# A fused attention and feed-forward kernel: output tiles of the last block brought forward, evictions shared, eight transposing loads

## Chip, cores, metric

One NeuronCore of a Trainium2 chip. The metric is the device time of the core in microseconds (us), lower is better. A "tail" below is the time from the end of the last exponential on ScalarE to some later event.

## What is computed

x is 2048 x 512 in bf16. There are 32 heads of size 16, and a feed-forward width of 1792.

```python
g = sigmoid((x * gate_w).sum(-1, keepdims=True))
a = attention(x, wqkv) @ wo                      # softmax(q k^T / 4) v, 32 heads
b = (silu(x @ w_gate) * (x @ w_up)) @ w_down
out = g * a + (1 - g) * b
```

## The kernel before: the parts concerned

The kernel orders the instructions of TensorE (PE), VectorE (DVE) and ScalarE (ACT) at build time, by planned costs. Of every 16 key tiles in a "unit" (four heads, 512 queries) most go to ScalarE as exponentials, and some to VectorE, which computes exp with arithmetic on bit patterns (y_t). The kernel uses eight banks of PSUM: two pairs for scores, one for o_ps (the product with v), three for everything else.

```python
# loads: nine transposing DMAs
parts = [(0, 2 * QBW, dc) for dc in range(DC)] + [(2 * QBW, S, dc) for dc in range(DC - 1)]
parts += [(2 * QBW, 3 * QBW, DC - 1), (3 * QBW, S, DC - 1)]
for t0, t1, dc in parts:
    nc.sync.dma_start_transpose(out=xT[:, dc, t0:t1], in_=x[t0:t1, dc * P:(dc + 1) * P])
# ...
def gate_end():
    act(out=ge[:, :], in_=ge[:, :], func=ACT.Tanh, scale=0.5)
    def end():                                   # gval = g, omg = 1 - g
        vec.tensor_scalar(out=gval[:, :], in0=ge[:, :], scalar1=1.0, scalar2=0.5, op0=ALU.add, op1=ALU.mult)
        vec.tensor_scalar(out=omg[:, :], in0=ge[:, :], scalar1=-0.5, scalar2=0.5, op0=ALU.mult, op1=ALU.add)
    later(0.4, end, plan.act + 0.2)              # 0.4: the planned cost
# ... in down_pieces: bblk = omg * (feed-forward product)
# ... in next_pv: emit_pv(pv_list(None)[0])      # ScalarE blocks first, then y_t blocks

def tail(k):       # k = 0: just ahead of the last product with v; k = 1: behind it
    if k == 0:
        a_ps.extend(m_tile("a_l")[:, :] for _ in range(2))
        al = ps_s.tile([P, 2 * QBW], F32, tag="s", name="al")
        a_ps.extend([al[:, 0:QBW], al[:, QBW:2 * QBW]])
    todo = [(tq, b) for tq in range(TQ) for b in range(NB - 1)]        # 12 products
    for tq, b in todo[:11] if k == 0 else todo[11:]:
        mm(a_ps[tq][:, 0:D], lhsT=onc[QB - 1][:, b, tq * P:(tq + 1) * P], rhs=wo_t[:, b, :], ...)
# ... the end of the program
tail(1)
last_mm(0, osbs[un - 1])        # four products
# dt: sums of the last unit's heads; reciprocal; rps: broadcast; on_l = osb * rps
last_mm(1, on_l)                # four products
for tq in range(TQ):            # mt = a_ps * gval + bblk on VectorE, then a store on SP
    store((QB - 1) * TQ + tq, a_ps[tq], bblk[:, tq, :], mt[:, tq, :])
```

## Time and profile before

| | before |
|---|---|
| median of the first three runs | 847.9 us (847.81 to 848.98) |
| span of the profiled execution | 846.8 us |
| first exponential starts / last one ends | 18.66 / 834.92 us |
| tail, last exponential's end to the end | 11.9 us |

The end of the last exponential is the start and duration of the last `e_t` line of the timeline.

```profile
833.69 1.23 ACT L160 ACTIVATE e_t<-s_t 128x1024 bf16<-128x1024 f32 x1
...
833.64 1.17 ACT L160 ACTIVATE e_t<-s_t 128x1024 bf16<-128x1024 f32 x1
```

The profile is to be read with this in mind: between 18.66 and 834.92 ScalarE is busy nearly throughout (800.48 of the 808.40 us from 18.60 to 827.00), so only the head, the tail and the small idle times of ScalarE can give anything.

### The profile page before, as it was taken

The numbers are of one execution on the slowest core, as the hardware profiler recorded it, in microseconds if no ns is written. First come the engines' busy times: TensorE is split into PE (matmuls) and PEld (weight loads), VectorE is DVE, ScalarE is ACT, GpSimd is POOL, SyncE is SP. The second block draws the span as 40 slices with busy tenths as digits, with TensorE's granted clock in tenths as the row PEclk, the third lists the DMA queues.
The fourth block names the chain that finished last, engine by engine and source line by source line (L and its number), as shares of the span: only waits on it lengthen the run. The fifth ranks groups of instructions, "written<-read, shape, count | busy, mean of one in ns | idle before, by whom it ended". The sixth has DMA issues, their size and how long they took to land. (4 is left out here: it accounts for less than half of the span.)

```text
span 846.8 us, 16228 instructions
## 1 busy us (share of the span) xinstructions
PE 764.1 (90%) x6049; PEld 262.5 (31%) x6078; DVE 797.4 (94%) x1160; ACT 813.9 (96%) x910; POOL 93.2 (11%) x122
## 2 busy tenths in 40 slices
PE   7999998999889998889899988898999899989995
PEld 3222233332223333232223322223333223233332
DVE  6999998999999999999999898999998999999995
ACT  3999999999999999999999999999999999999994
POOL 5010100010011011011101000100100110110100
PEclk9999999999999999999999999999999999999999
DMA  9432445345454334454443354444532554553331
GB/s 202 128 66 47 88 77 113 69 93 104 94 112 99 66 80 100 102 113 92 100 99 72 77 115 86 100 102 84 112 73 55 106 110 92 108 105 76 75 66 36
DMA packets 101447, 78.23 MB, mean 92 GB/s; under 512 B 77792, under 2 KB 89656, under 8 KB 101368
## 3 DMA queue, kind: packets, MB, share of 16 engines
q0 software_dynamic: 12672, 46.14, 28.6%
q1 hardware_dynamic: 87112, 30.86, 15.4%
q8 instruction: 47, 0.77, 0.4%
q10 hardware_dynamic: 1584, 0.20, 0.2%
q14 instruction: 32, 0.26, 0.1%
HBM read 20.83 MB, written 2.34 MB: 27 GB/s over the span
## 5 line engine op out<-in xcount | busy, mean ns | idle before, releaser
L160 ACT ACTIVATE e_t<-s_t 128x1024 bf16<-128x1024 f32 x846 | 791.9, 1106 | 8.3 <-PE s_t L157 6.6
L157 PE MATMUL s_t<-qx,kaug 64*128 64x512 bf16 x1376 | 293.9, 381 | 37.7 <-ACT e_t L160 32.5
L166 DVE TENSOR_SCALAR y_t<-d_t 128x512 uint16<-128x512 f32 x356 | 234.6, 682 | 15.8 <-PE d_t L157 13.2
L157 PEld LDWEIGHTS <-kaug 64*128 64x128 bf16 x2048 | 137.0, 93 | 323.8 <-issue 287.9
L157 PE MATMUL o_ps<-e_t,vaug 128*32 128x512 bf16 x1692 | 160.0, 389 | 2.3 <-DVE osb L166 1.0
L157 PE MATMUL gu_a<-xT,wg 64*128 64x512 bf16 x448 | 136.5, 377 | 0.0
L157 PE MATMUL gu_b<-xT,wu 64*128 64x512 bf16 x448 | 134.7, 377 | 1.3 <-DVE y_t L166 0.9
L157 PE MATMUL d_t<-qx,kaug 64*128 64x512 bf16 x288 | 107.6, 378 | 16.3 <-DVE y_t L166 9.2
L157 PEld LDWEIGHTS <-vaug 128*32 128x32 bf16 (+1 forms) x2148 | 46.0, 93 | 148.0 <-issue 146.6
L772 POOL DMA_DIRECT2D y_t<-u_t x44 | 40.1, 912 | 351.7 <-PE s_t L157 211.3
L772 POOL DMA_DIRECT2D y_t<-kaug x38 | 35.9, 946 | 310.3 <-PE s_t L157 191.4
L157 PE MATMUL dps_a<-wd_t,mt 64*128 64x512 bf16 x224 | 65.3, 376 | 0.0
L157 PE MATMUL dps_b<-wd_t,mt 64*128 64x512 bf16 x224 | 64.9, 375 | 0.3 <-DVE y_t L166 0.2
L166 DVE TENSOR_SCALAR z_t<-y_t 128x2048 uint16<-128x2048 uint16 x89 | 61.5, 691 | 2.1
L166 DVE TENSOR_SCALAR y_t<-y_t 128x2048 uint16<-128x2048 uint16 x89 | 60.9, 684 | 2.4 <-DMA y_t<-kaug 1.4
L166 DVE TENSOR_TENSOR u_t<-u_t 128x2048 f16<-128x2048 f16 x44 | 53.8, 1223 | 1.1
L166 DVE TENSOR_TENSOR u_t<-u_t,z_t 128x2048 f16<-128x2048 f16 x44 | 53.5, 1217 | 0.1
L157 PE MATMUL s_t<-q,kaug 64*128 64x512 bf16 x212 | 43.0, 381 | 7.6 <-ACT e_t L160 7.0
L166 DVE TENSOR_TENSOR kaug<-kaug 128x2048 f16<-128x2048 f16 x39 | 47.7, 1223 | 0.9
L166 DVE TENSOR_TENSOR kaug<-kaug,z_t 128x2048 f16<-128x2048 f16 x39 | 47.5, 1218 | 0.1
L157 PEld LDWEIGHTS <-wg 64*128 64x128 bf16 x448 | 40.8, 94 | 20.9 <-issue 9.0
L157 PEld LDWEIGHTS <-wu 64*128 64x128 bf16 x448 | 41.7, 94 | 16.1 <-issue 0.7
(119 smaller groups left out, 626.6 us busy)
## 6 DMA issues: line engine op xcount, KB each, us to landing
y_t<-u_t POOLq DMA_DIRECT2D x44, 512.0 KB, 4.8
y_t<-kaug POOLq DMA_DIRECT2D x38, 512.0 KB, 5.0
wg<-in_B_w_gate_dram SPq DMA_DIRECT2D x56, 128.0 KB
wu<-in_B_w_up_dram SPq DMA_DIRECT2D x56, 128.0 KB
y_t<-wd_t POOLq DMA_DIRECT2D x6, 512.0 KB, 4.6
on<-osb SPq DMA_DIRECT2D x120, 16.0 KB
rb<-rr SPq DMA_DIRECT2D x15, 128.0 KB
wd_t<-in_B_w_down_dram SPq DMA_DIRECT2D x7, 256.0 KB
```

Source lines behind the costliest of these rows:

```text
L157: return ordered(nc.tensor.matmul(*args, **kw))
L160: ordered(nc.scalar.activation(*args, **kw))
L166: return lambda *a, **kw: ordered(f(*a, **kw))
L772: nc.gpsimd.dma_start(out=ya, in_=ua, accum_op=ALU.add)
```

## The change

The intent is to shorten the serial tail. Output tiles 0 and 1 of the last block, with the feed-forward part added by a product with the identity matrix, go out while the last exponentials run. The last product with v is that of the last exponential and no longer a y_t product. Tiles 2 and 3 are split five and five around it. The gate is kept in another form, so that out = g * (a + ((1-g)/g) * b): now the eviction needs one PSUM operand and a scale only, which ScalarE can do too. The loads become eight of one size.

```diff
-    parts = [(0, 2 * QBW, dc) for dc in range(DC)] + [(2 * QBW, S, dc) for dc in range(DC - 1)]
-    parts += [(2 * QBW, 3 * QBW, DC - 1), (3 * QBW, S, DC - 1)]
+    for t0 in (0, 2 * QBW):
+        for dc in range(DC): ...                       # eight loads of 1024 rows
@@ gate_end
-        act(out=ge, in_=ge, func=ACT.Tanh, scale=0.5)
+        act(out=ge, in_=ge, func=ACT.Exp, scale=-1.0)  # ge = exp(-l), gval = 1 / (1 + ge), omg = ge * gval
-        later(0.4, end, plan.act + 0.2)
+        later(0.5, end, plan.act + 0.2)
@@ down_pieces: end
+            share = omg if qb < QB - 1 else ge
@@
+    def last_rows(t):
+        cs = slice(t * P, (t + 1) * P)
+        return lambda i: ((onc[QB - 1][:, i, cs], wo_t[:, i, :]) if i < NB - 1 else
+                          (osbs[UNITS - 2][:, cs], wo_l[:, 0, :]) if i == NB - 1 else (ident[:, :], bblk[:, t, :]))
+    def last_pieces():                                 # tiles 0 and 1: ten pieces of two half-row products
+        return two_banks(NB + 1, "a_l", last_rows(0), last_rows(1), keep, stop=False)
+    def tail(k):
+        todo = [(tq, i) for tq in (2, 3) for i in range(NB + 1)]
+        for tq, i in todo[:5] if k == 0 else todo[5:]: ...
@@ the chain is paced once all its inputs are there
+            pace.add(last_pieces(), SLOTS - KT // 2, SLOTS, prev, cond=ripe)
@@ next_pv
+        ns = pv_list(None)
+        if closed == UNITS - 1 and done_a[closed] == hi[closed] - 1 and vready:
+            ns.reverse()
+        emit_pv(ns[0])
@@ the end
-    for tq in range(TQ):
-        store((QB - 1) * TQ + tq, a_ps[tq], bblk[:, tq, :], mt[:, tq, :])
+        if tq % 2 == 0:
+            vec.tensor_scalar(out=mt[:, tq, :], in0=a_ps[tq][:, 0:D], scalar1=gval[:, t:t + 1], ...)
+        else:
+            act(out=mt[:, tq, :], in_=a_ps[tq][:, 0:D], func=ACT.Identity, scale=gval[:, t:t + 1])
+        (nc.sync if tq % 2 == 0 else nc.scalar).dma_start(out=out_f[...], in_=mt[:, tq, :])
```

More of the change, by code (lines that the diff above doesn't have):

```diff
@@ L171 @@
     xT = big.tile([P, DC, S], BF16, name="xT")
-    parts = [(0, 2 * QBW, dc) for dc in range(DC)] + [(2 * QBW, S, dc) for dc in range(DC - 1)]
-    parts += [(2 * QBW, 3 * QBW, DC - 1), (3 * QBW, S, DC - 1)]
-    for t0, t1, dc in parts:
-        nc.sync.dma_start_transpose(out=xT[:, dc, t0:t1], in_=x[t0:t1, dc * P:(dc + 1) * P])
+    for t0 in (0, 2 * QBW):
+        for dc in range(DC):
+            nc.sync.dma_start_transpose(out=xT[:, dc, t0:t0 + 2 * QBW], in_=x[t0:t0 + 2 * QBW, dc * P:(dc + 1) * P])
     wqk = big.tile([P, DC, 2 * D], BF16, name="wqk")
@@ L377, in sync, with two_banks @@
                           reason="row halves of one bank")
-    def two_banks(n, name, a, b, end):
+    def two_banks(n, name, a, b, end, stop=True):
         st = {}
@@ L396, in f @@
                     st["half"] = mm(ps[:, :], lhsT=w[rows, :], rhs=r[rows, :], start=(k == i == 0),
-                                    stop=(k == 2 * n - 1), tile_position=(64 * h, 0), skip_group_check=True)
+                                    stop=(stop and k == 2 * n - 1), tile_position=(64 * h, 0), skip_group_check=True)
                 spend("R", 1)
@@ L602, in end @@
             def end():
-                vec.tensor_copy(out=ge[:, t0:t0 + 2], in_=gp[:, t0:t0 + 2])
+                vec.tensor_scalar(out=ge[:, t0:t0 + 2], in0=gp[:, t0:t0 + 2], scalar1=-60.0, scalar2=60.0,
+                                  op0=ALU.max, op1=ALU.min)
                 m_free(gp, plan.dve)
@@ L608, in gate_end @@
     def gate_end():
-        act(out=ge[:, :], in_=ge[:, :], func=ACT.Tanh, scale=0.5)
+        act(out=ge[:, :], in_=ge[:, :], func=ACT.Exp, scale=-1.0)
         plan.act += 0.2
         def end():
-            vec.tensor_scalar(out=gval[:, :], in0=ge[:, :], scalar1=1.0, scalar2=0.5, op0=ALU.add, op1=ALU.mult)
-            vec.tensor_scalar(out=omg[:, :], in0=ge[:, :], scalar1=-0.5, scalar2=0.5, op0=ALU.mult, op1=ALU.add)
-        later(0.4, end, plan.act + 0.2)
+            vec.tensor_scalar(out=omg[:, :], in0=ge[:, :], scalar1=1.0, scalar2=None, op0=ALU.add)
+            vec.reciprocal(gval[:, :], omg[:, :])
+            vec.tensor_tensor(out=omg[:, :], in0=ge[:, :], in1=gval[:, :], op=ALU.mult)
+        later(0.5, end, plan.act + 0.2)
     def gu_chain(qb, fc):
@@ L648, in gu_chain @@
         return load, two_banks(DC, "gu", rows("g"), rows("u"), done_gu)
+    scaled = set()
     def down_pieces(qb, tq):
@@ L660, in end @@
             n = qb * TQ + t
-            vec.tensor_scalar(out=bblk[:, t, :], in0=p[:, 0:D], scalar1=omg[:, n:n + 1],
+            share = omg if qb < QB - 1 else ge
+            vec.tensor_scalar(out=bblk[:, t, :], in0=p[:, 0:D], scalar1=share[:, n:n + 1],
                               scalar2=None, op0=ALU.mult)
+            if qb == QB - 1:
+                scaled.add(t)
             m_free(p, plan.dve)
@@ L917, in store, with keep @@
         nc.sync.dma_start(out=out_f[t * P:(t + 1) * P, :], in_=o_t)
+    here_done = []
+    a_ps = []
+    def last_rows(t):
[3 more added lines that the diff above has]
+    def last_pieces():
+        def keep(pa, pb):
+            a_ps.extend([pa, pb])
+        return two_banks(NB + 1, "a_l", last_rows(0), last_rows(1), keep, stop=False)
+    def tail(k):
+        if k == 0:
+            assert here_done and len(scaled) == TQ
+            for c in list(pace.chains):
+                force(c)
+            al = ps_s.tile([P, 2 * QBW], F32, tag="s", name="al")
+            a_ps.extend([al[:, 0:QBW], al[:, QBW:2 * QBW]])
+        todo = [(tq, i) for tq in (2, 3) for i in range(NB + 1)]
+        for tq, i in todo[:5] if k == 0 else todo[5:]:
+            w, r = last_rows(tq)(i)
+            mm(a_ps[tq][:, 0:D], lhsT=w, rhs=r, start=(i == 0), stop=False)
     def fin_pieces(qb, tq):
@@ L972 @@
     k0_evict(0)
-    for dc in range(DC):
-        if dc < DC - 1:
-            for tb in (2, 3):
-                k0(dc, tb)
+    for dc in range(DC - 1):
+        for tb in (2, 3):
+            k0(dc, tb)
         if dc == 0:
             v0(0)
-        elif dc < DC - 1:
+        else:
             keep_warm(3)
@@ L1080, with ripe @@
         if last:
+            def ripe():
+                return (all((qb, b) in normed for b in range(NB - 1)) and len(scaled) == TQ and here_done)
+            pace.add(last_pieces(), SLOTS - KT // 2, SLOTS, prev, cond=ripe)
             break
@@ L1112, in part @@
                         m_free(here[un][0], plan.dve)
+                        here_done.append(un)
                 later(1.2, part)
@@ L1197, in put_piece @@
         pace.credit -= emit_piece(c)
-    a_ps = []
-    def last_mm(w, on):
-        for tq in range(TQ):
-            mm(a_ps[tq][:, 0:D], lhsT=on[:, tq * P:(tq + 1) * P], rhs=wo_l[:, w, :], start=False, stop=(w == 1))
-    def tail(k):
-        if k == 0:
-            assert all((QB - 1, b) in normed for b in range(NB - 1))
-            a_ps.extend(m_tile("a_l")[:, :] for _ in range(2))
-            al = ps_s.tile([P, 2 * QBW], F32, tag="s", name="al")
-            a_ps.extend([al[:, 0:QBW], al[:, QBW:2 * QBW]])
-        todo = [(tq, b) for tq in range(TQ) for b in range(NB - 1)]
-        for tq, b in todo[:11] if k == 0 else todo[11:]:
-            mm(a_ps[tq][:, 0:D], lhsT=onc[QB - 1][:, b, tq * P:(tq + 1) * P], rhs=wo_t[:, b, :],
-               start=(b == 0), stop=False)
     def next_pv():
@@ L1229, in next_pv @@
                 emit_d()
-        emit_pv(pv_list(None)[0])
+        ns = pv_list(None)
+        if closed == UNITS - 1 and done_a[closed] == hi[closed] - 1 and vready:
+            ns.reverse()
+        emit_pv(ns[0])
     SLACK = 0.1
@@ L1355 @@
     tail(1)
-    last_mm(0, osbs[un - 1])
     dt = m_tile("dt")
@@ L1371 @@
         vec.tensor_tensor(out=on_l[:, cs], in0=osb[:, cs], in1=rps[:, cs], op=ALU.mult)
-    last_mm(1, on_l)
     for tq in range(TQ):
-        store((QB - 1) * TQ + tq, a_ps[tq], bblk[:, tq, :], mt[:, tq, :])
+        mm(a_ps[tq][:, 0:D], lhsT=on_l[:, tq * P:(tq + 1) * P], rhs=wo_l[:, 1, :], start=False, stop=True,
+           skip_group_check=tq < 2)
+    for tq in range(TQ):
+        t = (QB - 1) * TQ + tq
+        if tq % 2 == 0:
+            vec.tensor_scalar(out=mt[:, tq, :], in0=a_ps[tq][:, 0:D], scalar1=gval[:, t:t + 1], scalar2=None, op0=ALU.mult)
+        else:
+            act(out=mt[:, tq, :], in_=a_ps[tq][:, 0:D], func=ACT.Identity, scale=gval[:, t:t + 1])
+        (nc.sync if tq % 2 == 0 else nc.scalar).dma_start(out=out_f[t * P:(t + 1) * P, :], in_=mt[:, tq, :])
 _INS = ['A_x', 'A_wqkv', 'A_wo', 'B_x', 'B_w_gate', 'B_w_up', 'B_w_down', 'gate_w']
```

## The prediction

> **What bounds the kernel now.** I read first the page's busy shares and costliest groups, then the busy time by stretch, then the chain that ended last, then the timeline of the last and the first microseconds. The costliest group is ScalarE's exponentials. There are 32 x 16 x 4 = 2048 score blocks of 128x512; ScalarE takes them two at a time, 846 instructions or 1692 blocks, and VectorE takes the other 356 (89 groups of four).
>
> ```profile
> L160 ACT ACTIVATE e_t<-s_t 128x1024 bf16<-128x1024 f32 x846 | 791.9, 1106 | 8.3 <-PE s_t L157 6.6
> L166 DVE TENSOR_SCALAR y_t<-d_t 128x512 uint16<-128x512 f32 x356 | 234.6, 682 | 15.8 <-PE d_t L157 13.2
> ```
>
> Idle before those 846 instructions is 8.3 us in all: ScalarE is full from the first score to the last. The stretches show what stands outside:
>
> ```profile
> 0.00:18.60 18.60, 14.97 (x112) 7.18 (x113) 11.84 (x34) 5.53 (x7) 10.92 (x34) 1.00 0.92 197
> 18.60:827.00 808.40, 737.57 (x5842) 251.07 (x5868) 774.62 (x1110) 800.48 (x895) 82.24 (x88) 1.00 0.44 92
> 827.00:835.00 8.00, 5.83 (x56) 1.78 (x53) 6.50 (x8) 7.92 (x9) 0.00 (x0) 1.00 0.01 3
> 835.00:847.00 12.00, 5.72 (x45) 2.43 (x45) 4.47 (x10) 0.00 (x0) 0.00 (x0) 0.92 0.13 44
> ```
>
> The columns are busy us of PE, PEld, DVE, ACT and POOL, then clock, DMA share and GB/s. In the last 12 us ScalarE does nothing: that is the tail, latency alone. From 827 to 835 VectorE and the PE have room (the timeline shows the PE filling it with dummy products `o_ps<-xT,vaug`). The chain that ended last (start, us, what) says the tail is one serial path:
>
> ```profile
> 832.78 0.80 ACT e_t L160
> 833.65 1.28 ACTq L1401
> 835.52 1.24 PE a_l L157 x5
> 836.76 1.08 PE al L157 x5
> 840.25 0.88 DVE on_l L166 x4
> 841.13 0.66 DVE mt L166
> 841.79 0.66 DVEq L1401
> 842.45 1.32 DVE mt L166 x2
> ```
>
> and the timeline gives its order on the engines:
>
> ```profile
> 834.97 0.39 PE L157 MATMUL o_ps<-e_t,vaug 128*32 128x512 bf16 x2 [0.52 <-ACT e_t L160]
> 835.52 1.24 PE L157 MATMUL a_l<-wo_t,on 128*128 128x512 bf16 x5 [0.16 <-issue]
> 836.60 1.24 PE L157 MATMUL al<-wo_t,on 128*128 128x512 bf16 x5
> 837.77 0.40 PE L157 MATMUL o_ps<-y_t,vaug 128*32 128x512 bf16 x4
> 838.23 0.69 DVE L166 CAST osb<-o_ps 128x512 bf16<-128x512 f32 x1 [4.59 <-PE o_ps L157]
> 839.20 0.24 PE L157 MATMUL dt<-sel_t,osb 128*128 128x4 bf16 x4
> 841.82 2.31 SPq L917 DMA_DIRECT2D out_dram<-mt  x4
> ```
>
> The last exponential ends near 834.92 and its product with v starts at 834.97. But eleven products of the output projection follow, and only then the last product with v, that of a VectorE block (y_t) that had been ready since 833.63. So the copy of o_ps waits to 838.23, and everything after it.
>
> [...] So scaling a PSUM tile should cost what scale-and-add costs; the trace agrees: bblk<-dps_a 745 ns, mt<-a_l 744 ns. The saving at the end is in sharing the four between two engines, not in a cheaper operation. [...] The trace has one table load (1.28 us) although exp, tanh and identity alternate, so the new Exp for the gate and Identity at the end should load nothing. [...] the four stores go out at VectorE's pace, 841.82 to 844.13, and I count only the earlier issue. [...] In the trace the weight load for o_ps after another mode has 0.42 us idle before it; I keep those gaps as they stand between the same neighbours.
>
> **The change, part by part.**
>
> *A, the order of the last products.* Before, after the last exponential the PE does 11 + 4 (v) + 1 + 4 products before dt. After, output tiles 0 and 1 (contraction of four blocks plus the identity product) go out earlier as ten pieces of two half-row products; the y_t product is put ahead of the last ScalarE tile; only five products of tile 2 stand before the last v product and five of tile 3 after it. A product of 512 columns costs 0.216 us ((836.60 - 835.52) / 5). The ten pieces cost 10 x 0.216 = 2.2 us of PE time, half-rows running in pairs. They fit from 827.3 (last bblk of the last group, 826.58 + 0.74) to 833.7: seven exponentials at 0.91, each taking a score pair of 0.22 and on average one v group of 0.22 plus a mode change; I estimate 0.3 us free in each, 2.1 us, and the dummies make way. So they fit narrowly and at zero cost.
> Then: y_t product about 833.7 (ready 833.63), issue 0.22, a gap of 0.2, five products 1.08, a gap of 0.1: the last v product starts about 835.3, already past the last exponential (834.92). Before it started at 837.77. The gain is 2.45 us. Against the ideal of 834.97 (2.8 us) it is 0.35 less, since the five products reach past the exponential.
> From that start to dt the path is the same length: before 837.77 to 839.20 = 1.43, holding five products; after also five. Reciprocal, broadcast and on_l are unchanged, so everything up to the four evictions moves by 2.45.
>
> *B, the evictions and stores.* Before: four on VectorE, 841.13 to 843.77, 0.66 apart; last store issued at 843.8. After: VectorE does two (841.13 to 842.45 on the old clock), ScalarE two. A ScalarE read of 128x512 from PSUM took 0.59 us (q0r, aq, vaug). It can start at about 841.25 (a_l of tile 1 at 840.82 + 0.38), ends 841.85, its queue spends about 0.5 on the store (0.97 for two at the start of the program), the second eviction runs 842.4 to 843.0. So the last store is issued at 843.05 and not 843.8: gain 0.7 us. What follows it (to 846.8, 3.0 us) is unchanged.
>
> *C, the eight loads.* Nine transposing loads hold the SP queue 12.03 us, 1.3 each, the half-size ones too. Eight save 1.3 us of issue. But the first exponential hangs on this:
>
> ```profile
> 14.29 0.38 PE L157 MATMUL kp<-xT,mt 128*128 128x512 bf16 x1
> 15.45 0.38 PE L157 MATMUL kp<-xT,mt 128*128 128x512 bf16 x1 [0.78 <-DVE kpart L166]
> ```
>
> The first of the two comes right behind three warm-up products (13.64 + 3 x 0.216 = 14.29), the second waits for VectorE's maximum over the other half. Neither is set by the ninth load (a weight load at 14.44 is the only thing that saw it). One load of both halves comes between the old eighth and ninth. I put this at 0, with 0.2 either way.
>
> *D, the gate.* One more tiny VectorE operation (about 0.2 us, as the 166 ns of gval), one Exp for one Tanh: nothing on a path. Its planned cost goes from 0.4 to 0.5, though, and the order of all three engines is worked out at build time from such costs. So nearly everything after 170 us may be ordered a little differently. The number of blocks that VectorE takes is whole; a group more or less is two exponentials, 2 x 0.915 = 1.83 us on ScalarE. I expect 89 again, at about 0.75.
>
> Sum: 2.45 + 0.7 + 0 = 3.15 us. 847.9 - 3.15 = 844.7.
>
> **Rivals.** *R1, the reshuffle decides.* A plan with 88 groups costs 1.8 us, one with 90 gains it, and idle before exponentials can move from its 8.3 us by half a microsecond or so. For it: VectorE is 94% busy and admits a block by a threshold. Against: ScalarE stays full in any such plan, so the end moves by little else. It would make 842.9 or 846.5. *R2, the new chain does not fit ahead.* If the last scaling comes later, or the plan gives the ten pieces no room, what is left is forced before the last v product, 0.22 us each; all ten would take 2.2 us of the gain and make 846.9. For it: my 2.1 us of room against 2.2. Against: the dummies show real room, and between the last score and 834 there is more. *R3, the new ScalarE eviction is slower than counted* (a store issue that blocks longer, or the tile waiting for both halves): the end is set by VectorE's or ScalarE's second store and B shrinks to 0.2, making 845.2. *R4, the merged load comes late* and moves the first exponential by up to 0.6 us: 845.3.
>
> **Range and chances.** A and B are short, measured chains: I give them 0.5 us of spread. R1 is the larger: 1.2 us. Together about 1.3; eight in ten is 1.7 to either side, with a little more above for R2: 842.9 to 846.6. Two per cent is 17 us; nothing here can reach it, so faster 0.01, same 0.985, slower 0.005.
>
> **What would show it.** Right: o_ps<-y_t ahead of the last o_ps<-e_t; osb's copy within 0.9 us of the last exponential's end (3.3 before); half-row a_l products between 827 and 834 and fewer dummies; last eviction to end still 3.0 us; 846 exponentials; first exponential within 0.2 us of 18.66. Wrong: a count other than 846, or a last exponential away from 834.9 by over 1 us (R1); a_l pieces after 834 (R2); a ScalarE eviction ending after VectorE's second by over 0.8 us (R3); a first exponential after 19.0 (R4).

## More of the kernel before

The runs e1 to e4, e5 to e8 and e9 to e12 were made on three different chips, each time beside the kernel before; ratios may be compared across them, single times less well.

## The result and the profile after

844.0 us median of four runs (843.76 to 844.9) against 848.05 us of before in the same rounds (847.81 to 848.98). The ratio is 0.9952, 95% interval 0.9935 to 0.9969. Ratios here are the mean time of one kernel's fast runs over that of the other's of the same rounds, so not quite the ratio of the medians quoted. The time lies in the stated range, 0.7 us below the stated 844.7, and within 2% of before, as forecast.

The page of the kernel after, its two costliest groups of ScalarE and VectorE work:

```profile
L160 ACT ACTIVATE e_t<-s_t 128x1024 bf16<-128x1024 f32 x846 | 791.9, 1103 | 8.2 <-PE s_t L157 6.2
...
L166 DVE TENSOR_SCALAR y_t<-d_t 128x512 uint16<-128x512 f32 x356 | 234.4, 680 | 16.4 <-PE d_t L157 13.5
```

The counts 846 and 356 are unchanged and the idle time is 8.2 us (8.3 before): the long middle is nearly the same program (e6 says how nearly). The difference is behind it. The chain that ended last, kernel after (start, us, what):

```profile
831.84 1.15 ACT e_t L160
834.38 0.81 PE al L157 x3
835.51 1.19 PE al L157 x5
837.59 0.88 DVE on_l L166 x4
838.47 0.66 DVE mt L166
839.13 0.67 DVEq L1429
839.82 0.69 ACT mt L160
```

The timeline of the same stretch, kernel after:

```profile
833.58 0.39 PE L157 MATMUL o_ps<-y_t,vaug 128*32 128x512 bf16 x4
...
833.95 0.81 PE L157 MATMUL al<-wo_t,on 128*128 128x512 bf16 x2
...
835.12 0.40 PE L157 MATMUL o_ps<-e_t,vaug 128*32 128x512 bf16 x4
...
835.57 0.69 DVE L166 CAST osb<-o_ps 128x512 bf16<-128x512 f32 x1 [2.05 <-PE o_ps L157]
...
836.54 0.24 PE L157 MATMUL dt<-sel_t,osb 128*128 128x4 bf16 x4
...
838.58 0.69 ACT L160 ACTIVATE mt<-a_l_b,gval 128x512 bf16<-128x512 f32 x1 [3.76 <-PE a_l_b L157]
839.05 0.74 DVE L166 TENSOR_SCALAR mt<-al,gval 128x512 bf16<-128x512 f32 x1
...
839.82 0.69 ACT L160 ACTIVATE mt<-al,gval 128x512 bf16<-128x512 f32 x1 [0.56 <-DVE mt L166]
840.54 0.36 ACTq L1402 DMA_DIRECT2D out_dram<-mt  x1
```

The last exponential ends at 834.81 (833.64 + 1.17). The y_t product comes before it, and the last product with v starts 0.31 us after it, where it was 2.85 us before. The copy of o_ps follows at once. From there to dt the path has its old length (1.42 us). At the end ScalarE's second eviction shows a wait of 0.56 us for VectorE, which had read the other half of the same PSUM tile `al`.

Three events, in us from the end of the last exponential, carry the whole comparison. They come out of the timelines in the same way for every run, and, unlike the whole time, they hardly vary between executions of the same program (two profiles of each here).

| kernel | last v product | on_l | last store issued | from there to the end |
|---|---|---|---|---|
| before | 2.85 | 5.33 | 8.87 | 3.01 |
| before, again (e10) | 2.86 | 5.34 | 8.88 | 3.05 |
| after | 0.31 | 2.78 | 5.73 | 2.66 |
| after, again (e1) | 0.29 | 2.77 | 5.72 | 2.61 |

So the change took 3.14 us out of the path up to the last store's issue: 2.55 up to on_l and 0.59 between on_l and the store. The last column is not the change's doing: it took the values 2.57 to 2.68 or 2.97 to 3.10 in all fourteen profiles, on both sides (e11 below is the kernel before with 2.60, e4 the kernel after with 3.10).

### The profile page after: what moved, and what is told of

Same layout as the page of the kernel before. A ratio compares the mean times of both kernels' runs of the same rounds, so it can differ in the third digit from the quotient of the medians.

```text
span 843.2 us, 16224 instructions
## 1 busy us (share of the span) xinstructions
PE 763.7 (91%) x6047; PEld 263.8 (31%) x6076; DVE 795.7 (94%) x1159; ACT 815.1 (97%) x912; POOL 93.2 (11%) x122
```

## The experiments

My theory, T: the time goes with the tail alone, each 512-column product that stands between the last exponential and the last v product costs its 0.216 us, and sharing the evictions gives 0.6. Rival L: something besides the tail, such as the loads, adds to it, as the medians differ by 4.05 us and not 3.14. Rival R1 of the prediction: the order that the plan finds decides. Each of the twelve kernels was timed in five rounds against the kernel before; all results were correct.

**e1, the changed kernel again.** No edit.

> The changed kernel again, as the yardstick for the other runs of this call. From the two traces I expect 3.2 us less than before from the tail up to the last store's issue (2.65 by the earlier last v product, 0.58 by the shared evictions), plus 0.35 between the last store's issue and the end (3.0 before, 2.66 after), so 3.6; the first four runs gave 4.05 between medians. Theory T (the tail alone): 3.4 to 4.1 us. Rival L (something besides the tail, such as the loads, adds to it): stays at 4.05 or more while the last exponential ends within 0.2 us of before.

844.29 us median, ratio 0.9948 (0.9926 to 0.9969). The tail repeats to 0.01 us up to the store. The time from the first exponential to the end of the last was 814.8 us here and 816.0 in the first profile: this middle varies between executions of one program by more than the amount in dispute. Part of the reason stands in the traces: the granted clock of TensorE drops to 0.50 for 3.41 us at a time in the middle too, from 524.13 us in the profile of before, from 255.30 and from 548.85 us in the kernel after, from 546.72 us in e1, nowhere in e9. In the three such stretches of before and after ScalarE was busy for 2.37, 2.98 and 2.38 of the 3.41 us, where its mean share gives 3.38. Among the runs of one kernel the slow ones have the lower mean clock: in e5 0.988 in the two near 851.3 and 852.0 us, 0.994 to 0.998 in the other four. Why their number differs is not shown. The median difference (3.9) does not by itself decide between T and L; e4, e10 and e11 were for that.

**e2, y_t last.** The order of the last two v products undone:

```diff
         if closed == UNITS - 1 and done_a[closed] == hi[closed] - 1 and vready:
-            ns.reverse()
+            pass
```

> The changed kernel with the last two v products in their old order (y_t last). Theory T: the product of the last exponential starts at about 834.87, then five products of 0.216 and the y_t product, which starts at about 836.3 against 835.12; so the end is 1.2 us later than the changed kernel's. Rival (the order is worth nothing, the paced chain alone made the gain): no later than 0.2 us.

847.79 us median, ratio 0.9990 (0.9970 to 1.0010): nearly the whole gain is gone, three times what T says. The timeline of this run:

```profile
834.80 0.39 PE L157 MATMUL o_ps<-e_t,vaug 128*32 128x512 bf16 x2 [0.52 <-ACT e_t L160]
...
836.35 0.63 PE L157 MATMUL al<-wo_l,osb 128*128 128x512 bf16 x1
836.78 0.63 PE L157 MATMUL al<-bblk,ident 128*128 128x512 bf16 x1
837.34 0.62 PE L157 MATMUL o_ps<-y_t,vaug 128*32 128x512 bf16 x4
```

The products follow each other at 0.43 us (836.35 to 836.78), twice the usual. The busy time by stretch of this run has the reason (columns as in the prediction; the clock is the third number from the end):

```profile
831.78:835.19 3.41, 1.98 (x17) 0.65 (x14) 1.65 (x2) 2.97 (x4) 0.00 (x0) 1.00 0.00 0
835.19:838.60 3.41, 3.19 (x11) 0.89 (x12) 0.59 (x1) 0.00 (x0) 0.00 (x0) 0.50 0.00 0
```

The granted clock of TensorE fell to half just as the tail began, for 3.41 us. In the microseconds before it the PE had been busy 0.43, 0.81 and 0.48 us (832 to 835). In the kernel after it was 0.39, 0.97 and 0.95, in the kernel before 0.94, 0.72 and 0.42, and in both the clock stayed at 1.00. The mean clock was 0.991 to 0.995 in all six executions of e2 and 0.995 to 0.999 in those of e1, so the fall was hardly that of the profiled one alone. That the clock fell for lack of activity was a guess at this point; e9 tests it.

**e3, all evictions on VectorE.** The four last evictions and stores:

```diff
-        if tq % 2 == 0: vec.tensor_scalar(...)
-        else: act(...)
-        (nc.sync if tq % 2 == 0 else nc.scalar).dma_start(...)
+        vec.tensor_scalar(out=mt[:, tq, :], in0=a_ps[tq][:, 0:D], scalar1=gval[:, t:t + 1], ...)
+        nc.sync.dma_start(...)
```

> The changed kernel with all four last evictions on VectorE and all four stores on SP; the identity product stays. Theory T: the last store is issued 0.58 us later than in the changed kernel, as evictions follow at 0.66 us; the end 0.5 to 0.9 us later. Rival (sharing the evictions gains nothing because the four stores' data bound the end): under 0.2 us.

The last store is issued 6.32 us after the last exponential, 0.59 later than in the kernel after; the median is 844.92 us, 0.63 above e1. As T says. The ratios (0.9951 against 0.9948) do not separate the two; the trace does.

**e4, nine loads in the changed kernel.** The first hunk of the diff undone.

> The changed kernel with the nine transposing loads of before. Theory T: the second half's first product stands behind warm-up products and the rest behind VectorE's maximum, so the first exponential is within 0.2 us and the time within 0.3 us of the changed kernel. Rival L: the merged load carries the 0.4 to 0.9 us that the tail does not explain, so this run is that much slower.

First exponential at 18.67 us, against 18.83 and 18.85 with eight loads; last store issued at 5.72. Median 844.87 us, 0.58 above e1, ratio 0.9964 (0.9939 to 0.9988). The profile is T's, the median is at the lower edge of L's; e11 asks again from the other side.

**e5, the order alone in the kernel before.** The `ns.reverse()` hunk put into the kernel before, nothing else.

> The kernel before with nothing but the y_t product put ahead of the last ScalarE block's product; eleven products of the output still stand before the last v product. The y_t product runs at about 833.6, eleven products of 0.216 from 833.95 reach to about 836.35, the last v product starts at about 836.4 against 837.77. Theory T (each product ahead of the last v product past the last exponential costs 0.216 us): gain 1.35 us. Rival (the order alone is the whole 2.65): 2.4 us or more.

The last v product starts 1.59 us after the last exponential instead of 2.85, and the last store is issued at 7.61 instead of 8.87: 1.26 us gained, by T 1.35. The rival (the order is worth all of it) is out. The median, 847.86 against 848.01, shows none of this, because the middle of this profile was 817.3 us and the runs scattered from 846.2 to 852: a microsecond must be read in the trace here. Order and chain thus share the gain: 1.26 for the order with eleven products still in the way, and 1.28 more (1.59 to 0.31) for having five in the way and not eleven. Six products fewer at 0.216 are 1.30.

**e6, the plan disturbed by the gate.** In the kernel before only:

```diff
-        later(0.4, end, plan.act + 0.2)
+        later(1.0, end, plan.act + 0.2)
```

> The kernel before with only the planned cost of the gate's end set to 1.0 instead of 0.4 (the change set it to 0.5). The instructions are the same; some 4300 lines of the PE's order and 400 of VectorE's differ from before, where 0.5 alone moves 28. Still 89 groups on VectorE. If ScalarE's exponentials are the bound whatever the order (theory): within 0.8 us of before. Rival R1 (the order of the plan is worth microseconds): 1 us or more, either way.

850.32 us median, 2.3 above before, ratio 1.0023 (0.9998 to 1.0047); 846 exponentials; tail 8.88 up to the store, as before; middle 817.5 us. That is over my 0.8 us and on R1's side, though the interval touches 1. The change itself set the cost to 0.5. By the order of instructions as built, 0.5 alone moves 28 of some 12,150 lines on the PE, near the gate itself; then the plan is back on its old course. With the rest of the change the PE's order differs there and from 826.8 us on only. (The expectation's "the instructions are the same" is not quite so: e6 as built has 48 more PE lines.)

**e7, an attempt to go on.** Tile 3 in its own PSUM bank, dt in a free half of the tile rps, and the ten products of tiles 2 and 3 split in four places:

```diff
-            al = ps_s.tile(...); a_ps.extend([al[:, 0:QBW], al[:, QBW:2 * QBW]])
-        todo = [(tq, i) for tq in (2, 3) for i in range(NB + 1)]
-        for tq, i in todo[:5] if k == 0 else todo[5:]:
+            a3 = m_tile("a3"); al = ps_s.tile(...); a_ps.extend([al[:, 0:QBW], a3])
+        todo = [(tq, i) for tq in (3, 2) for i in range(NB + 1)]
+        cut = (0, 4, 7, 8, 10)      # ahead of the last v product, beside the copy, the reciprocal, the scaling
+        for tq, i in todo[cut[k]:cut[k + 1]]:
```

> An attempt to go on: of the ten products of tiles 2 and 3, four stand before the last v product (they end with the last exponential), three beside the copy of o_ps, one beside the reciprocal, two beside the scaling; tile 3 gets its own PSUM bank and dt shares a tile with rps. Theory T: last v product at 834.87 against 835.12, dt right after the copy at about 836.05 against 836.54, and the second ScalarE eviction no longer waits 0.12 us for VectorE's read of the shared tile: 0.5 to 0.6 us faster than the changed kernel. Rival (mode changes of the PE eat it): 0.2 us or less.

The timeline of e7:

```profile
835.25 0.40 PE L157 MATMUL o_ps<-e_t,vaug 128*32 128x512 bf16 x4
...
836.45 0.25 PE L157 MATMUL rps<-sel_t,osb 128*128 128x4 bf16 x4
...
839.09 0.68 ACT L160 ACTIVATE mt<-a,gval 128x512 bf16<-128x512 f32 x1
839.22 0.94 ACTq L1406 DMA_DIRECT2D out_dram<-mt  x2
```

The last exponential ends at 835.18, so the last v product now starts 0.07 us after it (the four products ahead of it end at about the same time), on_l starts at 2.33 instead of 2.78, and the last store is issued at 4.62 instead of 5.73: 1.11 us gained where I expected 0.5 to 0.6. The 0.45 up to on_l are as expected. The other 0.66 come from ScalarE's second eviction: it no longer waits for VectorE, and the queue issues stores beside it. I had read that wait as costing 0.12 us, taking the store issue as the other limit, but the issue did not hold the engine (above, a store is issued from 839.22, within the eviction of 839.09 to 839.77). The median is 843.9 us, ratio 0.9944 (0.9923 to 0.9964). That is the lowest but one of all, yet its interval overlaps the changed kernel's: only the trace separates them.

**e8, stores moved too.** As e7, with tile 1's store issued by SP.

> As the run before, with the store of tile 1 issued by SP and not by ScalarE, so that ScalarE's two evictions follow each other. ScalarE's issue took 0.37 us plus waits between them, so its second eviction ends some 0.5 us earlier; the SP issues three at 0.36. The last store is issued 0.3 us earlier, or somewhat less as 4 x 128 KB at about 340 GB/s are 1.55 us of data. Expect 0.2 to 0.4 us faster than the run before. Rival (data bound): none.

The last store is issued at 4.97, 0.35 later than in e7: three stores in SP's order now end the row (the last from 840.63, 0.40 us). Median 843.6 us, ratio 0.9942 (0.9922 to 0.9961), not to be told from e7. My expectation missed: the issue beside ScalarE's work was free already. The stores of the kernel after moved at 337 GB/s from 840.05 to 841.10 (about 340 in the expectation).

**e9, e2 with the PE kept busy.** Dummy products of zero weights before the last exponential's end:

```diff
-                    w for t, w in work_at[-24:] if t > plan.pe - 3.0) < 6.5:
+                    w for t, w in work_at[-24:] if t > plan.pe - 3.0) < (14.0 if plan.slot >= SLOTS - 4 else 6.5):
+        # and, once, five groups of the same dummies ahead of the last but one v product
```

> e2 (old order of the last two v products in the changed kernel) with dummy products of zero weights put into the idle PE time between 831 and 834.7, none behind the last exponential. In e2 the products behind the last exponential came at 0.43 us and the granted clock read 0.5 to 0.6 from 835 to 838; its tail from the last exponential's end to the end was 11.25 us against 8.39 and 8.33. Theory K (the clock was lowered because the PE had little work from 832 to 835, 0.39 to 0.81 us busy of each us): the clock stays at 1.00, the products come at 0.216, the tail is 8.4 + 1.2 = 9.6 us, 1.6 less than e2. Rival (the clock fell for another reason, such as the first full-width products after a wait): tail stays near 11.2.

The stretches and the y_t product of e9 (its last exponential ended at 835.17):

```profile
835.00:836.00 1.00, 1.00 (x11) 0.32 (x5) 0.00 (x0) 0.16 (x1) 0.00 (x0) 1.00 0.00 0
836.00:837.00 1.00, 1.00 (x8) 0.28 (x6) 0.00 (x0) 0.00 (x0) 0.00 (x0) 1.00 0.00 0
```

```profile
836.72 0.40 PE L157 MATMUL o_ps<-y_t,vaug 128*32 128x512 bf16 x4
```

Clock 1.00 until after the last store is issued, last v product 1.55 us after the last exponential (2.59 in e2), last store at 6.98 (8.57), tail 9.63 against 9.6 expected. Median 846.56 us, ratio 0.9981 (0.9969 to 0.9994). So e2's surplus of 1.6 us was the clock, and in these two profiles the clock followed the PE's load in the microseconds ahead (in e9 the dummies keep it busy for 1.25 us from 833.93; the expectation's 0.39 is the kernel after's; e2's lowest was 0.43): more useless work made the tail shorter (9.63 us against 11.25). The intervals of the two ratios overlap, so the whole times alone do not show it. Nor is the share of busy time the whole rule: in e9 a stretch of the same length, 520.39 to 523.80 us, was busy for 1.91 us, and in the kernel before the one from 20.00 to 23.41 us for 1.77 us, both less than e2's 1.98, and the clock stayed at 1.00. At full clock the order is worth 1.25 us in the changed kernel too (6.98 - 5.73).

**e10, the kernel before against itself; e11, only the eight loads in the kernel before.** No edit, and the first hunk of the diff.

> The kernel before against itself: a test of the spread. In the profiles of the kernels so far the time from the first exponential to the end of the last was 814.8 to 816.7 us for seven executions with the changed kernel's order, 816.3 and 817.3 for two with the order of before. Expect ratio 1 within 0.25 percent, tail 11.9, and a middle anywhere from 814.8 to 817.3. If the rest of the gain (some 0.5 us beyond the tail) is noise, this middle is about as often below 816.0 as above; rival L: it is above 816.2 again.

> The kernel before with nothing but the eight transposing loads. Theory T: no effect, first exponential 18.5 to 19.0, tail 11.9, time within 0.5 us of before. Rival L (the loads carry what the tail does not explain): 0.5 to 1.3 us faster than before, with a middle under 816.

e10: 848.0 us, ratio 1.0001 (0.9989 to 1.0014), middle 815.5 us. e11: 848.13 us, ratio 0.9999 (0.9985 to 1.0013), first exponential 18.50 us, middle 816.4, last store at 8.87. The loads alone give nothing that shows, though the interval leaves room for about 1 us, and the middle of before can be under 816 as well. So no run speaks for rival L, but only the trace speaks against it. Middles with the order of before: 816.3, 817.3, 815.5, 816.4 (mean 816.4); with the changed kernel's: 816.0, 814.8, 816.2, 816.4, 815.4, 816.5, 816.7, 815.5 (mean 815.9). The means differ by less than the spread of either.

**e12, one group fewer on VectorE.** In the kernel before only:

```diff
-    ADD_US = 6.0
+    ADD_US = 5.5
```

> The kernel before with the planned time of the accumulating DMA at 5.5 us instead of 6.0; the plan then gives VectorE 88 groups and ScalarE 848 exponentials. It tests the size given to R1 in the prediction: one group less costs ScalarE 2 x 0.915 = 1.83 us, so middle about 818, time 1 to 2.5 us above before. Rival (other waits of the new order are larger than a group): outside that.

The page of e12:

```profile
L160 ACT ACTIVATE e_t<-s_t 128x1024 bf16<-128x1024 f32 x848 | 794.8, 1132 | 6.0 <-PE s_t L157 4.8
```

848 exponentials, as planned, but 845.08 us median, ratio 0.9970 (0.9957 to 0.9982): faster than before, where I expected 1 to 2.5 us slower. The middle is 813.8 us, 2.4 under that of before, with two exponentials more; idle before the exponentials is 6.0 us instead of 8.3. The tail is 7.38 up to the store, since this order happens to have its last y_t product early, as e5. So the size of R1 was wrong in sign: the waits that an order brings weigh more than a group. The start times in the traces say where the 2.4 us and the 1.8 of the two added exponentials came from. Two exponentials in a row start 0.904 us apart at the median, and what they start later than that adds up to 23.5 us in before (and in e10) and to 19.9 in e12, which is 3.6 less; the other 0.7 us, at exponentials behind a `th` (the tanh of the feed-forward part), is in the first profile of before and not in e10. Why this order delays them less is open. The same setting in the changed kernel gives, as built, 89 groups and another order, so the two gains don't simply add; I have not run it.

## Why the prediction was right, and where it was off

**The bound.** Right: ScalarE's 846 exponentials stayed, with 8.2 us idle, and the change acted behind them.

**A, the order of the last products: 2.45 us expected, 2.54 measured** at the last v product (2.85 to 0.31), 2.55 at on_l. The y_t product came at 833.58 (I said 833.7) and the last v product at 835.12 (835.3), past the exponential by 0.31, as the five products ahead of it end later than the exponential does (the last of them starts at 834.81, when it ends). e5 and e9 show the two shares, and e7 removes the rest.

**The ten pieces.** Expected to fit narrowly; they fitted well: a_l products from 826.83 to 831.2; the first started before the last scaling of bblk had ended (827.21), since only the last pieces need it. R2 did not come up. Fewer dummies came too: 84 products and not 100, the last at 760 us where before they ran to 832.6. What I had not seen is what that can do to the clock: in e2, with no dummies behind the pieces and the y_t product left for the tail, the PE was busy for 1.98 of the 3.41 us ahead of it and the clock fell to 0.50, at a cost of 1.6 us by e9. That the change as made escaped this was luck.

**B, evictions and stores: 0.7 expected, 0.59 measured**, and e3 gives the 0.59 back. The gain was in the sharing: on VectorE the scale alone took 742 ns, scale-and-add 744 ns before. The mis-sized terms: ScalarE's eviction took 0.69 us and not 0.59, since my 0.59 came from reads of another form (Copy 597 ns and Abs 592; Identity with a scale per partition 687); and its second one waited until 839.82, not for the store issue that I had counted (0.37) but for VectorE's read of the shared tile. That was R3's second half, "the tile waiting for both halves", in part; e7 shows it to be worth 0.66 with a tile of its own.

**C, the loads: 0 expected.** e4's first exponential and e11's ratio of 0.9999 (0.9985 to 1.0013) agree. The first exponential came at 18.83 in the profile after (18.66 before), within the 0.2 I had given. With eight loads it was also 18.50 to 19.66 in other runs, so this is scatter.

**D and R1.** No table load came with the gate's Exp or with Identity at the end: both profiles have one, of 1.28 us at 2.4 us. The count stayed at 89 as expected, because a cost of 0.1 us moved few instructions, 28 lines of the PE's order by itself, where I had said that nearly everything after 170 us might move. But the reason I gave for R1's size, that ScalarE is full in any plan so that a group is worth 1.83 us, fell with e12 and e6: orders differ by 2 us either way through waits. The range held because the plan came back to its old course, not because my size was right: for R1 that was luck.

**The sum.** 3.15 us expected up to the last store, 3.14 measured. The two paths were the right ones; that the sum agrees to 0.01 is luck, since A came 0.10 larger and B 0.11 smaller. "Unchanged" for the stretch after it was right only on average: 3.01 and 2.66 in the two profiles, a scatter of both kernels. The medians differ by 4.05 us in the first rounds; 3.14 is inside the interval of the ratio (2.6 to 5.5 us from 848.05). Whether the remaining 0.9 is all scatter of the middle, the clock's drops included, and of the stores is not settled; e10 and e11 found no other source.

## What to carry to other kernels

When one engine is full to its last instruction, look at what stands between that and the end, in the order of each engine's queue: put work whose inputs were ready long before ahead of the full engine's last result, and behind that result only what depends on it. Measure such a change from a fixed event in the trace, since microseconds drown in the scatter of whole runs. And take care what moving work away does to the clock: in e2, with a lighter PE ahead of a latency-bound tail, the clock fell to 0.50 for 3.41 us and the tail took 11.25 us, against 9.63 with the PE kept busy (e9).

## What the runs leave open

- The load at which the granted clock falls. In e2 it fell though the PE was busy for 1.98 of the 3.41 us before; with 1.91 of 3.41 us in e9 and 1.77 in the kernel before it did not.
- Why ScalarE's reads of 128x512 from PSUM differ: Copy and Abs took 597 and 592 ns here, and Identity with a per-partition scale 687 ns.
- Why the time from the last store's issue to the end of the program took two values in these fourteen profiles, near 2.6 and near 3.05 us, for the same kernels.
